# Causal masks by GpSimd affine select, one-column denominator weights, six product groups and a contiguous second quad, in a fused attention and MLP kernel

## The chip, the cores and the metric

The kernel runs on one core of a Trainium2 chip. The metric is the device time of one execution in microseconds (us); less is better. A time is the median of the runs of one kernel. A profiled execution has a span about 1.7 us shorter than its device time (before: 380.64 us and 378.9 us), so stage lengths below, which come from traces, add up to the span. On one core no second state could be told apart; every profiled run that is used here was classed fast.

The engines in the profile are PE (TensorE matmuls), PEld (TensorE weight loads), DVE (VectorE), ACT (ScalarE), POOL (GpSimd) and SP (SyncE, which issues most loads here). PSUM is the memory that TensorE writes its products to, SBUF the memory of everything else on the core.

## The reference, cut to what matters

```python
batch, n_heads, seq, head_dim = 8, 8, 576, 64        # f is in [0.8, 1.0)
def _attn_ref(q, k, v, f):
    scores = scale * q @ k^T                          # per batch and head
    cum = np.cumsum(np.log(np.clip(f, 1e-4, 1.0)), axis=-1)
    scores = np.where(causal, -1e9, scores + cum[..., :, None] - cum[..., None, :])
    attn = exp(scores - max);  attn = attn / sum(attn)
    return attn @ v
x = attention output as [4608, 512]                   # tokens by (head, dim)
h = x @ w_in                                          # w_in [512, 2048]
return gelu_tanh(h) @ w_out                           # w_out [2048, 512]
```

(Shortened; the mask, the decay and the division are as in the reference.)

## The kernel before: the parts that the change and the argument touch

The 64 heads are handled as 16 *quads* of four heads, two quads to a batch. A quad goes through four *rounds* of scores. In each, TensorE multiplies a strip of keys by queries, ScalarE takes the exp of it and writes it to `pt`, and the diagonal block of the strip is masked. The decay is folded into weights `w = exp(-cum)` of the keys: `vw = v * w` for the value product, `w` alone for the denominator. While quad `i` makes scores, the quad before it, `j`, makes its denominators and its two value products `po`, which VectorE multiplies by the reciprocal denominators into `xT`. Between these pieces, TensorE is kept busy with output matmuls of the MLP (`pull(fill, n)` pulls n of them). After every batch comes a block of MLP input matmuls (`mlp_in`) with Gelu on ScalarE.

```python
    rounds = [(0, [(0, 0, 400)]),
              (400, [(0, 400, 176), (3, 384, 192)]),
              (768, [(1, 128, 448)]),
              (1216, [(2, 256, 320), (4, 512, 64)])]
    po_parts = [(0, 256, 256), (256, 576, 512)]       # the product is cut where PSUM banks end
    # psS has 2 buffers of [128, 1024] FP32, psO has 1, psM has 2 of [128, 512]

    def make_vw(i):                                   # both on GpSimd
        nc.gpsimd.tensor_mul(vw[i % 2], v_nat[...], wT[:, i, :, :] ...broadcast)
        nc.gpsimd.tensor_copy(wrep[i % 2], wT[:, i, :, :] ...broadcast to 32 columns)

    def mask(i, r):                                   # of each diagonal block in round r
        nc.vector.tensor_mul(p[:, :, o:o + w], p[:, :, o:o + w], utri[:, :, :w] ...broadcast)

    def denominators(i):
        po = product(i, [... 32 equal columns of wrep for each head ...])
        nc.vector.transpose(out=den, in_=po)
        for x in range(2):
            nc.vector.reciprocal(rec[x], den[:, 0:S:32])
        for x in range(2):
            for g in (0, 64):                         # a head's rows to its neighbour's
                src, dst = g + 32 * x, g + 32 - 32 * x
                nc.vector.tensor_copy(rec[x][dst:dst + 32, :], rec[x][src:src + 32, :])
        # ... (cut) two transposes spread rec[x] to rb[x]

    def attn_out(i, x):                               # x: the pair of heads
        po = product(i, [... vw of two heads, 64 columns each ...])   # the one psO buffer
        nc.vector.tensor_mul(xT[b % 2][:, 2 * u + x, :], po, rbs.pop((i, x)))

    def step(i, j, fill, fills, n=None):              # i: scores, j: products, n: loads
        for r in range(4):
            # ... (cut) score_round(i, r): matmuls, two exps
            if j is not None and r > 0:
                if r == 1: denominators(j)
                else:      attn_out(j, r - 2)
            if r == 0:
                if n is not None: cast_k(n); cast_q(n)          # GpSimd
                if i is not None: make_vw(i)                    # GpSimd
            # ... (cut) transposes of k and q of quad n on VectorE in rounds 1 and 2
            if i is not None and r > 0: mask(i, r - 1)
            pull(fill, fills[r])
            if i is not None and r == 3: mask(i, 3)
```

The softmax here doesn't subtract the row's maximum and nothing guards it: scores larger than these inputs give would overflow.

## Time and profile before

Device time: 381.1 us, median of 3 runs (380.83 to 381.11).

The first thing to look at is how busy TensorE is in each stretch. The span falls into four: the start-up up to the end of the first MLP input block, the quads 2 to 4 up to the start of the second such block, the steady state up to the start of the last block, and the tail. This is the table of stretches of the kernel before: start and end, length, then busy time of each engine (with its number of instructions), the granted TensorE clock as a share of full speed, the share of the DMA engines, and GB/s.

```profile
core 0: us, PE busy (x) PEld busy (x) DVE busy (x) ACT busy (x) POOL busy (x), PEclk, DMA share, GB/s
0.00:61.43 61.43, 37.79 (x347) 24.25 (x348) 30.75 (x56) 27.39 (x37) 20.40 (x26) 0.92 1.12 191
61.43:92.58 31.15, 26.33 (x307) 12.32 (x314) 23.36 (x40) 21.56 (x27) 15.31 (x11) 0.95 0.81 170
92.58:340.21 247.63, 241.15 (x2373) 146.17 (x2401) 123.36 (x240) 146.59 (x197) 57.53 (x42) 1.00 0.44 97
340.21:378.90 38.69, 34.46 (x213) 20.95 (x214) 4.15 (x6) 10.32 (x16) 0.00 (x0) 0.98 0.11 41
```

TensorE is idle for 23.6 us of the first 61.4 (61.43 less 37.79), for 4.8 us of the next 31.2, and for 6.5 us of the long steady stretch. So the start-up holds the most that a change of order can win.

In the start-up the masks are the eye-catcher. These are two timelines of the kernel before, of VectorE and then of GpSimd (start, length, engine, line, operation, output and inputs, shapes, count; in brackets the idle time before it and what ended that).

```profile
19.13 0.63 DVE L193 TENSOR_TENSOR pt_91<-pt_91,utri 128x512 bf16<-128x512 bf16 x1
20.37 8.84 DVE L193 TENSOR_TENSOR pt_91<-pt_91,utri 128x512 bf16<-128x512 bf16 x4
```

```profile
20.38 2.34 POOL L160 TENSOR_TENSOR vw_89<-v_nat_83,wT 128x1280 bf16<-128x1280 f32 x1
22.66 0.93 POOL L163 CAST wrep_102<-wT 128x640 bf16<-128x640 f32 x1
...
25.84 2.36 POOL L160 TENSOR_TENSOR vw_90<-v_nat_83,wT 128x1280 bf16<-128x1280 f32 x1
28.12 0.95 POOL L163 CAST wrep_103<-wT 128x640 bf16<-128x640 f32 x1
```

Four masks take 8.84 us while GpSimd runs without a break (the cut line is its issue of three loads); one mask alone takes 0.38 us elsewhere. The Trainium skill, "GPSIMD Engine Reference", section 1. Specifications, says that GpSimd shares its SBUF interfaces with VectorE and contends with VectorE instructions of two SBUF inputs. A mask product has two SBUF inputs, and the trace agrees.

The end of the start-up is a serial piece with one PSUM tile. This is the timeline of all engines there:

```profile
41.39 0.72 DVE L242 TENSOR_TENSOR xT_93<-po,rb_463 128x576 bf16<-128x576 f32 x1
42.16 1.55 PE L208 MATMUL po<-pt_92,vw_90 128*64 128x256 bf16 x14 [1.75 <-DVE xT_93 L242]
43.74 0.76 DVE L242 TENSOR_TENSOR xT_93<-po,rb_465 128x576 bf16<-128x576 f32 x1 [1.64 <-PE po L208]
```

The second value product (at 42.16) can't start before the first multiply has read the only `po` tile, and the last `xT` is done at 44.50.

The table of waits (total us, times, longest) shows how long TensorE waited for such multiplies and for masks:

```profile
PE po L208 <- DVE xT_94 L242: 4.8, 6, 1.6
PE po L208 <- DVE xT_93 L242: 4.4, 3, 1.8
PE po L208 <- DVE pt_91 L193: 3.6, 3, 2.3
```

### The profile page before, as it was taken

Reading aid. Unit: us, or ns where it says so; the run is one execution under the profiler, and the core shown is the slowest. Engines: PE = TensorE matmul, PEld = TensorE weight load, DVE = VectorE, ACT = ScalarE, POOL = GpSimd, SP = SyncE. Lnnn points to the kernel's source line nnn. Section 1 sums busy time; section 2 is a strip of 40 time slices with the busy share of each in tenths; the row PEclk is TensorE's granted clock in tenths of the full one; section 3 lists DMA queues with packets and bytes.
Section 4 is the critical chain, followed back from the end, with each engine's and each line's share of the span. In section 5 each row is a group of like instructions: output and inputs, shape, how many; then the busy total and the mean of one; then the engine's idle time right before and its main releaser. Section 6 shows DMA issues by size and latency. Waiting matters only on the chain.

```text
span 378.9 us, 7775 instructions
## 1 busy us (share of the span) xinstructions
PE 339.7 (90%) x3235; PEld 203.7 (54%) x3273; DVE 181.6 (48%) x341; ACT 205.9 (54%) x276; POOL 93.2 (25%) x79
## 2 busy tenths in 40 slices
PE   0646698978999999999999999999999999899995
PEld 0214475435765467445754477446744576457742
DVE  4298502798307841396308840595128820760021
ACT  2744067746575556756674556655665557605500
POOL 1293115532501413050504131051406300000000
PEclk9999599989999999999999999999999999999999
DMA  9979999980692119911990239411911100010012
GB/s 186 204 113 195 216 221 219 229 189 29 161 205 67 57 57 222 153 50 39 213 190 29 83 101 220 93 49 67 226 18 55 57 29 0 29 57 28 2 55 83
DMA packets 86018, 42.59 MB, mean 112 GB/s; under 512 B 40352, under 2 KB 81312, under 8 KB 85984
## 3 DMA queue, kind: packets, MB, share of 16 engines
q1 hardware_dynamic: 79328, 36.73, 45.6%
q0 software_dynamic: 4224, 4.19, 7.0%
q10 hardware_dynamic: 2432, 1.18, 1.6%
q8 instruction: 25, 0.41, 0.5%
q14 instruction: 9, 0.07, 0.1%
HBM read 36.85 MB, written 9.44 MB: 122 GB/s over the span
## 4 chain that ended last, share of the span: by engine, by line
PE 75%; DVE 12%; issue 5%; DMA 4%; ACT 3%; SPq 0%; POOL 0%; ACTq 0%; POOLq 0%
PE ps_h L253 34%; PE pso L271 27%; PE po L208 9%; PE ps_s L175 5%; DVE pt_91 L193 2%; DMA v_nat_83<-in_v_dram 1%; DVE den L223 1%; DMA k_nat_80<-in_k_dram 1%; DVE xT_94 L242 1%; DVE pt_92 L193 1%; ACT pt_92 L184 1%; DMA k_nat_79<-in_k_dram 1%; DVE o_st L275 1%; ACT L184 1%; DVE xT_93 L242 1%
## 5 line engine op out<-in xcount | busy, mean ns | idle before, releaser
L271 PE MATMUL pso<-w_out_sb,gT 128*128 128x512 bf16 x538 | 129.2, 381 | 5.1 <-issue 4.6
L261 ACT ACTIVATE gT<-ps_h 128x576 bf16<-128x576 f32 x128 | 82.5, 651 | 75.9 <-PE ps_h L253 75.9
L253 PEld LDWEIGHTS <-w_in_sb 128*128 128x128 bf16 x1024 | 100.7, 98 | 29.5 <-issue 1.0
L271 PEld LDWEIGHTS <-gT 128*128 128x128 bf16 x576 | 51.6, 98 | 63.8 <-issue 8.4
L184 ACT ACTIVATE pt_91<-ps_s 128x800 bf16<-128x800 f32 (+3 forms) x64 | 50.1, 834 | 37.6 <-PE ps_s L175 30.0
L184 ACT ACTIVATE pt_92<-ps_s 128x800 bf16<-128x800 f32 (+3 forms) x64 | 50.1, 834 | 29.6 <-PE ps_s L175 21.6
L253 PE MATMUL ps_h<-xT_93,w_in_sb 128*128 128x288 bf16 x512 | 65.3, 289 | 0.5 <-ACT gT L261 0.5
L253 PE MATMUL ps_h<-xT_94,w_in_sb 128*128 128x288 bf16 x512 | 64.0, 286 | 0.1
L223 DVE STREAM_TRANSPOSE den<-po 128x576 f32<-128x576 f32 x16 | 12.5, 783 | 93.8 <-PE po L208 93.5
L275 DVE COPY o_st<-pso 128x512 f32<-128x512 f32 x36 | 24.7, 687 | 50.9 <-PE pso L271 46.4
L193 DVE TENSOR_TENSOR pt_92<-pt_92,utri 128x512 bf16<-128x512 bf16 (+1 forms) x40 | 30.9, 798 | 0.0
L193 DVE TENSOR_TENSOR pt_91<-pt_91,utri 128x512 bf16<-128x512 bf16 (+1 forms) x40 | 27.3, 718 | 4.6 <-ACT pt_91 L184 4.6
L147 POOL CAST k_bf<-k_nat_79 128x1152 bf16<-128x1152 f32 x8 | 9.2, 1148 | 80.5 <-DVE kT_88 L139 60.3
L175 PE MATMUL ps_s<-qT_85,kT_87 32*128 32x400 bf16 (+5 forms) x384 | 21.3, 299 | 7.6 <-DVE kT_87 L139 4.6
L175 PE MATMUL ps_s<-qT_86,kT_88 32*128 32x400 bf16 (+5 forms) x384 | 22.5, 294 | 2.7 <-DVE qT_86 L139 1.2
L160 POOL TENSOR_TENSOR vw_89<-v_nat_84,wT 128x1280 bf16<-128x1280 f32 x4 | 9.3, 2331 | 55.1 <-PE po L208 36.7
L175 PEld LDWEIGHTS <-kT_87 32*128 32x128 bf16 x384 | 8.1, 96 | 24.1 <-issue 17.7
L160 POOL TENSOR_TENSOR vw_89<-v_nat_83,wT 128x1280 bf16<-128x1280 f32 x4 | 9.3, 2335 | 45.2 <-PE po L208 36.1
L208 PE MATMUL po<-pt_91,vw_89 128*64 128x320 bf16 (+4 forms) x224 | 15.2, 278 | 5.1 <-DVE xT_94 L242 3.2
L208 PE MATMUL po<-pt_92,vw_90 128*64 128x320 bf16 (+4 forms) x224 | 15.3, 280 | 4.2 <-DVE xT_93 L242 1.8
L175 PEld LDWEIGHTS <-kT_88 32*128 32x128 bf16 x384 | 8.4, 95 | 19.4 <-issue 17.3
L208 PEld LDWEIGHTS <-vw_89 128*64 128x64 bf16 x224 | 11.5, 115 | 9.3 <-issue 8.4
(180 smaller groups left out, 230.2 us busy)
## 6 DMA issues: line engine op xcount, KB each, us to landing
out_dram<-o_st SPq DMA_DIRECT2D x36, 256.0 KB, 2.0
k_nat_79<-in_k_dram SPq DMA_DIRECT2D x32, 144.0 KB, 5.3
k_nat_80<-in_k_dram SPq DMA_DIRECT2D x32, 144.0 KB, 3.2
v_nat_84<-in_v_dram SPq DMA_DIRECT2D x16, 256.0 KB, 5.8
q_nat_77<-in_q_dram SPq DMA_DIRECT2D x28, 144.0 KB, 5.5
q_nat_78<-in_q_dram SPq DMA_DIRECT2D x28, 144.0 KB, 3.9
v_nat_83<-in_v_dram SPq DMA_DIRECT2D x12, 256.0 KB, 6.4
w_in_sb<-in_moe_w_in_dram POOLq DMA_DIRECT2D x4, 512.0 KB, 6.5
```

The source lines that it names most:

```text
L147: nc.gpsimd.tensor_copy(k_bf, k_nat[i % 2])
L160: nc.gpsimd.tensor_mul(vw[i % 2], v_nat[(i // QPB) % 2][:, :, h0:h0 + 4, :], wT[:, i, :, :].unsqueeze(3).to_broadcast([128, NT, 4, D]))
L175: nc.tensor.matmul(tiles[h // 2][:, h % 2, c0:c0 + nq], kk[32 * h:32 * h + 32, 128 * t:128 * t + 128, c], qq[32 * h:32 * h + 32, q0:q0 + n ...
L184: nc.scalar.activation(p[:, 2 * g:2 * g + 2, off:off + n], tiles[g][:, :, 0:n], AF.Exp, scale=scale)
L193: nc.vector.tensor_mul(p[:, :, o:o + w], p[:, :, o:o + w], utri[:, :, :w].to_broadcast([128, 4, w]))
L208: nc.tensor.matmul(po[r0:r0 + w.shape[-1], base + s - a:base + z - a], w, p[:, h, strip_off[t] + s - 128 * t:strip_off[t] + z - 128 * t], ...
L223: nc.vector.transpose(out=den, in_=po)
L242: nc.vector.tensor_mul(xT[b % 2][:, 2 * u + x, :], po, rbs.pop((i, x)))
L253: nc.tensor.matmul(ph[:, j, 0:hS], w_in_sb[:, dt, 128 * ft:128 * ft + 128], xT[b % 2][:, dt, hS * j:hS * (j + 1)], start=(dt == 0), stop=( ...
L261: nc.scalar.activation(gT[:, ft, o:o + S].rearrange("p (j n) -> p j n", j=2), ph[:, :, 0:hS], AF.Gelu_apprx_tanh)
L271: nc.tensor.matmul(pso, gT[:, ft, c:c + 128], w_out_sb[:, ft, :], start=(ft == 0), stop=(ft == N_FT - 1))
L275: nc.vector.tensor_copy(st, pso)
```

## The change

It takes the masks off VectorE (GpSimd makes them by affine select, which has one input), drops the 32-column weight copies `wrep` for one bf16 column per head, moves the denominators from round 1 to round 0, cuts a value product into six groups of matmuls in place of seven (64 + 512 columns in place of 256 + 320 at the bank boundary), gives the last start-up step a spare PSUM tile, and loads the second quad's k and q contiguously, cast to bf16 on the way, so that no cast is needed. The loads of quad 3 go ahead of v of batch 1. The diff, cut to its core:

```diff
-    po_parts = [(0, 256, 256), (256, 576, 512)]
+    Q0 = S - 512
+    po_parts = [(0, Q0, 512 - Q0), (Q0, S, 512)]
+    def load_contiguous(src, dst, i):            # one GpSimd DMA per tensor, FP32 to BF16
+    def transpose_contiguous(src, dst):          # (bodies cut)
 def make_vw(i): ...
-        nc.gpsimd.tensor_copy(wrep[i % 2], wT[:, i, :, :] ... [128, NT, 4, 32])
 def mask(i, r): ...
-                nc.vector.tensor_mul(p[:, :, o:o + w], p[:, :, o:o + w], utri[...])
+                nc.gpsimd.affine_select(
+                    out=p[:, :, o:o + w], in_=p[:, :, o:o + w], compare_op=ALU.is_ge,
+                    fill=0.0, base=0, pattern=[[0, 4], [1, w]], channel_multiplier=-1)
-    def product(i, groups):
-        po = psO.tile([128, 1024], FP32, name="po", tag="po")
+    def product(i, groups, spare):
+        if spare: po = psS.tile([128, 2, 512], FP32, name="ps_o", tag="s") ...
+        else:     po = psO.tile([128, 1024], FP32, name="po", tag="po")
 def denominators(i): ...
+        # weights: one column of w_bf, spread to 32 columns for t == 0 only
         for x in range(2):
+            rec = den_pool.tile([128, S // 32], FP32, ...)
+            nc.vector.reciprocal(rec, den[:, 0:S:32])
             for g in (0, 64):
-                nc.vector.tensor_copy(rec[x][dst:dst + 32, :], rec[x][src:src + 32, :])
+                nc.vector.tensor_copy(rec[dst:dst + 32, :], rec[src:src + 32, :])
             # then the transpose of this x into rb (before: after both pairs of copies)
 def step(...): ...
-            if j is not None and r > 0:
-                if r == 1: denominators(j)
-                else:      attn_out(j, r - 2)
+            if j is not None:
+                if r == 0:  denominators(j)
+                elif r > 1: attn_out(j, r - 2, spare=(i is None and r == 2))
...
-                fills = (11, 8, 8, 9) if b % 2 else (9, 6, 6, 7)
+                fills = (8, 11, 8, 9) if b % 2 else (6, 9, 6, 7)
```

(Cut: the setup's order of loads, two calls of `transpose_contiguous` and `make_vw(0)` in round 1 of the first step, the other fill counts, `load_qk(3)` moved up.)

More of the change, by code (lines that the diff above doesn't have):

```diff
@@ L73 @@
     ones_f32 = singles.tile([128, 128], FP32, name="ones_f32")
-    utri = singles.tile([128, 1, 128], BF16, name="utri")
     q_nat = many(2, [128, NA, 2, D], FP32, "q_nat")
@@ L82 @@
     kT = many(2, [128, SPAD, 2], BF16, "kT")
+    qk_c = many(2, [128, S // 32, D], BF16, "qk_c")
     vw = many(2, [128, NT, 4, D], BF16, "vw")
@@ L92 @@
     wT = singles.tile([128, NQ, NT, 4], FP32, name="wT")
-    wrep = many(2, [128, NT, 4, 32], BF16, "wrep")
+    w_bf = singles.tile([128, NQ, NT, 4], BF16, name="w_bf")
     shift = singles.tile([128, 1], FP32, name="shift")
@@ L144, in transpose_one @@
         )
+    def load_contiguous(src, dst, i):
+        b, h0 = i // QPB, 4 * (i % QPB)
+        return nc.gpsimd.dma_start(
+            out=dst.rearrange("p a d -> p (a d)"),
+            in_=src[b, h0:h0 + 4].rearrange("h (p a) d -> (h p) (a d)", p=32))
+    def transpose_contiguous(src, dst):
+        nc.vector.transpose(
+            out=dst[:, 0:S, :].rearrange("p s c -> p (s c)").bitcast(FP32)
+                .rearrange("p (t a) -> p a t", a=S // 32),
+            in_=src.rearrange("p a d -> p (a d)").bitcast(FP32)
+                .rearrange("p (a d) -> p a d", d=D // 2),
+        )
     def cast_k(i):
@@ L162, in make_vw @@
             wT[:, i, :, :].unsqueeze(3).to_broadcast([128, NT, 4, D]))
-        nc.gpsimd.tensor_copy(
-            wrep[i % 2], wT[:, i, :, :].unsqueeze(3).to_broadcast([128, NT, 4, 32]))
     def score_round(i, r):
@@ L192, in mask @@
                 w = min(128, nq)
-                nc.vector.tensor_mul(p[:, :, o:o + w], p[:, :, o:o + w],
-                                     utri[:, :, :w].to_broadcast([128, 4, w]))
-    def product(i, groups):
-        po = psO.tile([128, 1024], FP32, name="po", tag="po")
+                nc.gpsimd.affine_select(
+                    out=p[:, :, o:o + w], in_=p[:, :, o:o + w], compare_op=ALU.is_ge,
+                    fill=0.0, base=0, pattern=[[0, 4], [1, w]], channel_multiplier=-1)
+    def product(i, groups, spare):
+        if spare:
+            po = psS.tile([128, 2, 512], FP32, name="ps_o", tag="s").rearrange("p a n -> p (a n)")
+        else:
+            po = psO.tile([128, 1024], FP32, name="po", tag="po")
         p = pt[i % 2]
@@ L210, in product, with column, attn_out @@
                         p[:, h, strip_off[t] + s - 128 * t:strip_off[t] + z - 128 * t],
-                        start=(t == 0), stop=(t == (1 if z == 256 else 4)),
+                        start=(t == 0), stop=(t == (0 if z == Q0 else 4)),
                         skip_group_check=True,
                     )
-        return po[:, 256:256 + S]
+        return po[:, 512 - Q0:512 - Q0 + S]
     rbs = {}
     def denominators(i):
-        po = product(i, [(32 * g, lambda t, h=h: wrep[i % 2][:, t, h, :], h)
-                         for g, h in enumerate((0, 2, 1, 3))])
+        def column(h):
+            return lambda t: (w_bf[:, i, t, h:h + 1] if t else
+                              w_bf[:, i, t, h:h + 1].to_broadcast([128, 32]))
+        po = product(i, [(32 * g, column(h), h) for g, h in enumerate((0, 2, 1, 3))], False)
         den = den_pool.tile([128, S], FP32, name="den", tag="den")
         nc.vector.transpose(out=den, in_=po)
-        rec = [den_pool.tile([128, S // 32], FP32, name=f"rec{x}", tag=f"rec{x}") for x in range(2)]
         for x in range(2):
-            nc.vector.reciprocal(rec[x], den[:, 0:S:32])
-        for x in range(2):
+            rec = den_pool.tile([128, S // 32], FP32, name=f"rec{x}", tag=f"rec{x}")
+            nc.vector.reciprocal(rec, den[:, 0:S:32])
             for g in (0, 64):
                 src, dst = g + 32 * x, g + 32 - 32 * x
-                nc.vector.tensor_copy(rec[x][dst:dst + 32, :], rec[x][src:src + 32, :])
-        for x in range(2):
+                nc.vector.tensor_copy(rec[dst:dst + 32, :], rec[src:src + 32, :])
             rb = den_pool.tile([128, S], FP32, name=f"rb{x}", tag=f"rb{x}")
             nc.vector.transpose(out=rb.rearrange("p (c j) -> p c j", j=32),
-                                in_=rec[x].unsqueeze(2).to_broadcast([128, S // 32, 32]))
+                                in_=rec.unsqueeze(2).to_broadcast([128, S // 32, 32]))
             rbs[i, x] = rb
-    def attn_out(i, x):
+    def attn_out(i, x, spare=False):
         b, u = i // QPB, i % QPB
         po = product(i, [(64 * y, lambda t, h=2 * x + y: vw[i % 2][:, t, h, :], 2 * x + y)
-                         for y in range(2)])
+                         for y in range(2)], spare)
         nc.vector.tensor_mul(xT[b % 2][:, 2 * u + x, :], po, rbs.pop((i, x)))
@@ L286, in setup @@
         nc.sync.dma_start(out=f_sb, in_=f.rearrange("b h s -> (b h) s"))
-        load_heads(k, k_nat, 0, nc.sync)
+        k0 = load_heads(k, k_nat, 0, nc.sync)
         load_heads(q, q_nat, 0, nc.scalar)
         load_v(0, 0, 4)
-        load_heads(k, k_nat, 1, nc.sync)
         load_v(0, 4, 4)
@@ L293, in setup @@
         make_upper_triangular(nc, utri_f32, val=1.0, diag=True)
+        after(load_contiguous(k, qk_c[1], 1), k0[0])
+        load_contiguous(q, qk_c[0], 1)
         cast_k(0)
@@ L301, in setup @@
             nc.vector.memset(t_[:, S:SPAD, :], 0.0)
-        nc.vector.tensor_copy(utri[:, 0, :], utri_f32)
         nc.vector.tensor_scalar(f_sb, f_sb, 1e-4, 1.0, op0=ALU.max, op1=ALU.min)
@@ L306, in setup @@
         nc.scalar.activation(f_sb, f_sb, AF.Ln)
-        load_heads(q, q_nat, 1, nc.scalar)
         ps_lt = psM.tile([128, NT * BH], FP32, name="ps_lt", tag="m")
@@ L332, in make_w @@
                 AF.Exp, scale=-1.0, bias=shift[:rows, :])
+        nc.vector.tensor_copy(w_bf, wT)
     def pull(it, n):
@@ L350, in step @@
                     make_w()
-            if j is not None and r > 0:
-                if r == 1:
+            if j is not None:
+                if r == 0:
                     denominators(j)
-                else:
-                    attn_out(j, r - 2)
+                elif r > 1:
+                    attn_out(j, r - 2, spare=(i is None and r == 2))
             if r == 0:
@@ L361, in step @@
                     w_in_dmas.append(load_w_in(0))
-                if i is not None:
+                elif i is not None:
                     make_vw(i)
@@ L368, in step @@
                     transpose_q(n)
+            if i == 0 and r == 1:
+                make_vw(0)
+                transpose_contiguous(qk_c[1], kT[1])
+                transpose_contiguous(qk_c[0], qT[1])
             if i is not None and r > 0:
@@ L390 @@
         setup()
-        step(0, None, none, (0, 0, 0, 0), n=1)
+        step(0, None, none, (0, 0, 0, 0))
         w_in_dmas.extend(load_w_in(c) for c in range(1, 4))
@@ L395 @@
         step(1, 0, none, (0, 0, 0, 0))
+        load_qk(3)
         w_out_dmas = [load_w_out(c) for c in range(4)]
@@ L398 @@
         after(v1[0], w_out_dmas[1])
-        load_qk(3)
         step(None, 1, none, (0, 0, 0, 0))
@@ L419 @@
                 load_qk(5)
-                step(3, 2, fill, (7, 3, 3, 3), n=4)
+                step(3, 2, fill, (3, 7, 3, 3), n=4)
                 load_qk(6)
-                step(4, 3, fill, (6, 2, 2, 2))
+                step(4, 3, fill, (2, 6, 2, 2))
             elif b + 1 < B:
                 i = 2 * b + 3
-                fills = (11, 8, 8, 9) if b % 2 else (9, 6, 6, 7)
+                fills = (8, 11, 8, 9) if b % 2 else (6, 9, 6, 7)
                 pull(fill, 2)
@@ L430 @@
                 else:
-                    step(None, i, fill, (7, 6, 7, 7))
+                    step(None, i, fill, (6, 8, 6, 7))
         for x in fill:
```

## The prediction

> **What bounds the kernel now.** By stage (the table of stretches, PE busy of length): 0 to 43.6 us, start-up, PE 20.4 of 43.6; 43.6 to 61.5, first MLP-in, 17.4 of 17.9; 61.5 to 94, quads 2 to 4 between the first output tiles, 27.7 of 32.5; 94 to 342, steady state, about 97% (41.3 of 42.0, 39.6 of 41.0); 342 to 379, pure MLP tail. So after 94 us it is TensorE throughput, and what can be won lies before 94 us.
>
> Start-up, in the timeline: the second quad's k lands at 17.1, its scores start at 20.5. Then the five DVE masks of quad 0 end at 29.2 (four take 8.84 us, though one alone takes 0.38), because GpSimd is busy 9.98 of those 10 us. This agrees with the Trainium skill, "GPSIMD Engine Reference", section Specifications: GpSimd shares SBUF interfaces with VectorE and contends with instructions of two SBUF inputs, which a mask product is. The denominator matmuls wait for these masks and hold quad 1's round 2 until 29.44. After the last exp (34.4) the masks, denominator, two value products through one PSUM tile and two multiplies run in series until 44.5.
>
> **What changes.**
> 1. Masks go to GpSimd. The trace's own affine selects (0.23 us for 64 columns, 0.29 for 128) give an estimate of 0.5 to 0.75 us for 512 columns. DVE loses about 58 us busy; GpSimd gains about 50, loses 13.7 (weight copies). Start-up: quad 0's masks end at about 22 in place of 29.2, quad 1's last exp at about 30 in place of 34.4.
> 2. Spare PSUM tile: the second value product no longer waits 1.75 us for the multiply. Last xT at about 38 in place of 44.5: -6.5 us.
> 3. Contiguous loads: fewer, larger packets. Casting loads with larger pieces moved about 316 GB/s of source against 212 for the small-packet queue, so the 1.18 MB quad saves about 2 us of transfer; quad 1 is ready before PE wants it.
> 4. Six groups and one-column weights: successive product matmuls already start N/2.4 ns apart (320 columns 132 ns, 128 columns 52), weight loads are hidden. A product of seven groups takes 0.81 us against 0.67 for its 1600 columns. I expect 10 to 20 ns per product, 0.5 to 1 us in all.
> 5. Denominators one round earlier: the multiplies stop holding the PSUM tile. PE waits for xT (4.8 us after 61 us in the table of waits) mostly vanish: -3 us in 61 to 94, about -0.3 us a period later. GpSimd masks of round 3 now stand just ahead of the denominators: margin 0 to 0.4 us, so perhaps small new waits.
> 6. Quad 3's loads go ahead of v of batch 1. DMA runs without a break to 82 us; I expect v near 61 us, while MLP-in ends near 55. make_vw, and behind it on GpSimd the masks of quad 2, wait for it: about 1.5 us given back.
>
> **Sum:** -6.5 (start-up), -3+1.5 (quads 2 to 4), -2.5 (steady state), -0.7 (groups): about -11. Predicted 370.0 us, 80% range 365.0 to 374.5. Chances: faster by over 2% 0.84, within 2% 0.15, slower 0.01.
>
> **What the profile would show.** First MLP-in block done near 55 us (61.4 before); end of stage three near 84 to 86 (94); steady periods 0.3 to 0.6 us shorter; the tail still 37 us; affine selects about 0.7 us; PE waits on xT gone; PE waiting on masks near 66 us; product 0.79 to 0.81 us.
>
> **What would make it wrong.** Affine selects of 1 us or more, so that denominators wait in every round; first loads delayed because the contiguous ones stand ahead of the first GpSimd cast; DMA order starving v or the output weights by more than 2 us; or a colder clock in start-up.

## More of the kernel before

```profile
110.18 0.65 ACT L261 ACTIVATE gT<-ps_h 128x576 bf16<-128x576 f32 x1 [0.33 <-PE ps_h L253]
110.85 1.28 ACT L184 ACT_TABLE_LOAD   x1
112.15 1.57 ACT L184 ACTIVATE pt_92<-ps_s 128x800 bf16<-128x800 f32 x2
```

The table load of 1.28 us starts right after the last Gelu, without a wait. (The Trainium skill, "ScalarE: Activation LUTs", section What ACT_TABLE_LOAD costs, gives about 1283 ns for the load; the trace agrees.)

## The result

| | before | after |
|---|---|---|
| median, us | 380.99 (380.83 to 381.11, 4 runs) | 374.6 (374.07 to 375.21, 4 runs) |
| ratio to before | 1 | 0.9833 (95%: 0.9813 to 0.9853) |

A ratio here is the mean time of one kernel's fast runs over that of the other's fast runs of the same rounds, so it is not quite the ratio of the medians beside it. The kernel became 1.7% faster, which counts as the same at the 2% line. The prediction was 370.0 us, with a chance of 0.84 for more than 2%, and 374.6 lies just outside its range of 365.0 to 374.5.

This is the table of stretches of the kernel after, cut at the same events as before and with the same columns.

```profile
0.00:54.85 54.85, 36.60 (x331) 21.83 (x332) 23.01 (x46) 27.39 (x37) 23.87 (x35) 1.00 1.04 187
54.85:87.68 32.83, 27.26 (x292) 11.51 (x297) 16.41 (x28) 20.28 (x26) 17.11 (x19) 0.90 0.92 188
87.68:334.70 247.02, 241.49 (x2277) 140.44 (x2305) 95.33 (x182) 147.86 (x198) 82.43 (x90) 1.00 0.43 97
334.70:373.40 38.70, 34.52 (x214) 20.95 (x214) 4.15 (x6) 10.30 (x16) 0.00 (x0) 0.98 0.11 41
```

Set beside the prediction:

| stage | before, us | after, us | measured change | predicted change |
|---|---|---|---|---|
| start-up | 61.43 | 54.85 | -6.58 | -6.5 |
| quads 2 to 4 | 31.15 | 32.83 | +1.68 | -3 + 1.5 = -1.5 |
| steady | 247.63 | 247.02 | -0.61 | -2.5 - 0.7 = -3.2 |
| tail | 38.69 | 38.70 | 0 | 0 |
| span | 378.9 | 373.4 | -5.5 | -11.2 |

The start-up came out as predicted. The two middle stages are 3.2 and 2.6 us worse than predicted, and these 5.8 us are what has to be explained.

Now the lines that answer to those shown of before. The end of the start-up, in the timeline of all engines:

```profile
34.26 1.54 PE L227 MATMUL ps_o<-pt,vw 128*64 128x64 bf16 x12
35.62 1.50 PE L227 MATMUL po<-pt,vw 128*64 128x64 bf16 x12
38.08 0.72 DVE L264 TENSOR_TENSOR xT<-ps_o,rb 128x576 bf16<-128x576 f32 x1
38.72 0.74 DVE L264 TENSOR_TENSOR xT<-po,rb 128x576 bf16<-128x576 f32 x1
```

The two products now follow each other, and the last `xT` is done at 39.46 instead of 44.50.

From the table of waits, the one of TensorE for multiplies:

```profile
PE po L227 <- DVE xT L264: 5.3, 3, 2.9
```

The waits for masks are gone. Of the waits of the products (`po`) for `xT`, 9.2 us before (4.4 + 4.8), 5.3 are left. The same table by stage says where: in the start-up they fell from 4.4 to 2.4 us and in the steady stage from 2.0 to none, but in the stage of quads 2 to 4 they went from 2.8 us (1.6 and 1.2) to 2.9, in one piece. Around that one, in the stage of quads 2 to 4, the timeline of all engines shows:

```profile
67.72 1.15 POOL L166 CAST q_bf<-q_nat 128x1152 bf16<-128x1152 f32 x1
...
68.16 3.03 DVE L254 COPY rec<-rec 32x18 f32<-32x18 f32 x2
...
68.83 2.33 POOL L176 TENSOR_TENSOR vw<-v_nat,wT 128x1280 bf16<-128x1280 f32 x1
...
74.93 0.74 DVE L264 TENSOR_TENSOR xT<-po,rb 128x576 bf16<-128x576 f32 x1
...
75.72 1.55 PE L227 MATMUL po<-pt,vw 128*64 128x64 bf16 x12 [2.93 <-DVE xT L264]
```

In the kernel before, the same pair of copies came while GpSimd had nothing to do (it had been idle for 9.13 us when its next product started at 81.74), and took 0.35 us:

```profile
76.33 0.35 DVE L231 COPY rec_870<-rec_870 32x18 f32<-32x18 f32 x2
...
81.74 2.33 POOL L160 TENSOR_TENSOR vw_89<-v_nat_83,wT 128x1280 bf16<-128x1280 f32 x1 [9.13 <-DMA q_nat_77<-in_q_dram]
```

After, two copies of 32 x 18 numbers take 3.03 us. In the trace the first ends at 68.89, 0.02 us after the cast of q (67.72 + 1.15 = 68.87). The second runs from 68.90 to 71.19, and the product that makes `vw` ends at 71.16. Behind them the whole chain to the multiply at 74.93 is late, TensorE waits 2.93 us, and its clock drops: the value product after the wait takes 1.55 us, where the one at 70.34 took 0.87. The view by source line gives the spread of this copy's duration over the kernel (min/median/max in ns):

```profile
L254 DVE COPY rec<-rec x64: 164/171/2290, 24.6 to 329.8; 32x18 f32<-32x18 f32 x64
```

In the steady state, the timeline of ScalarE at the switch of its function table from Gelu to Exp:

```profile
105.28 0.65 ACT L283 ACTIVATE gT<-ps_h 128x576 bf16<-128x576 f32 x1 [0.33 <-PE ps_h L275]
106.44 1.28 ACT L198 ACT_TABLE_LOAD   x1 [0.50 <-PE ps_s L189]
107.73 0.84 ACT L198 ACTIVATE pt<-ps_s 128x800 bf16<-128x800 f32 x1
```

The load of the Exp table now starts 0.5 us after the last Gelu, only when the scores are there. Before, it started without a wait.

### The profile page after: what moved, and what is told of

Read it like the earlier page. It is cut to its first block, busy times and chain, and to the rows that moved or that the text cites. A ratio compares the mean times of both kernels' runs of the same rounds, so it can differ in the third digit from the quotient of the medians.

```text
span 373.4 us, 7488 instructions
## 1 busy us (share of the span) xinstructions
PE 339.9 (91%) x3108; PEld 194.7 (52%) x3145; DVE 138.9 (37%) x261; ACT 205.8 (55%) x276; POOL 123.4 (33%) x143
## 4 chain that ended last, share of the span: by engine, by line
PE 84%; DVE 6%; ACT 4%; issue 3%; DMA 2%; POOL 0%; ACTq 0%
PE ps_h L275 33%; PE pso L293 31%; PE po L227 9%; PE ps_s L189 9%; ACT pt L198 3%; DVE rec L254 2%; DMA k_nat<-in_k_dram 1%; DVE rb L256 1%; DVE xT L264 1%; DMA q_nat<-in_q_dram 1%; DVE den L247 1%; PE cum_ps L347 0%; DVE o_st L297 0%; ACT gT L283 0%; DVE rec L251 0%
## 5 line engine op out<-in xcount | busy, mean ns | idle before, releaser
L198 ACT ACTIVATE pt<-ps_s 128x800 bf16<-128x800 f32 (+3 forms) x128 | 100.2, 834 | 68.3 <-PE ps_s L189 66.0
L275 PE MATMUL ps_h<-xT,w_in_sb 128*128 128x288 bf16 x1024 | 128.2, 286 | 1.6 <-DVE xT L264 1.1
L208 POOL TENSOR_SCALAR_AFFINE_SELECT pt<-pt 128x512 bf16<-128x512 bf16 (+1 forms) x80 | 46.2, 591 | 158.0 <-ACT pt L198 156.3
L189 PE MATMUL ps_s<-qT,kT 32*128 32x400 bf16 (+5 forms) x768 | 44.7, 297 | 11.9 <-ACT pt L198 6.1
L176 POOL TENSOR_TENSOR vw<-v_nat,wT 128x1280 bf16<-128x1280 f32 x16 | 37.5, 2342 | 10.8 <-DMA v_nat<-in_v_dram 4.8
L264 DVE TENSOR_TENSOR xT<-po,rb 128x576 bf16<-128x576 f32 x30 | 22.7, 755 | 35.7 <-PE po L227 35.7
L227 PE MATMUL po<-pt,vw 128*64 128x64 bf16 (+1 forms) x360 | 28.9, 300 | 4.5 <-DVE xT L264 4.5
L227 PEld LDWEIGHTS <-vw 128*64 128x64 bf16 x384 | 17.2, 118 | 19.0 <-issue 13.0
L256 DVE STREAM_TRANSPOSE rb<-rec 128x576 f32<-128x576 f32 x32 | 24.9, 778 | 1.1
L254 DVE COPY rec<-rec 32x18 f32<-32x18 f32 x64 | 18.5, 290 | 1.5
```

What stands on the lines that cost most here:

```text
L176: nc.gpsimd.tensor_mul(vw[i % 2], v_nat[(i // QPB) % 2][:, :, h0:h0 + 4, :], wT[:, i, :, :].unsqueeze(3).to_broadcast([128, NT, 4, D]))
L189: nc.tensor.matmul(tiles[h // 2][:, h % 2, c0:c0 + nq], kk[32 * h:32 * h + 32, 128 * t:128 * t + 128, c], qq[32 * h:32 * h + 32, q0:q0 + n ...
L198: nc.scalar.activation(p[:, 2 * g:2 * g + 2, off:off + n], tiles[g][:, :, 0:n], AF.Exp, scale=scale)
L208: nc.gpsimd.affine_select(out=p[:, :, o:o + w], in_=p[:, :, o:o + w], compare_op=ALU.is_ge, fill=0.0, base=0, pattern=[[0, 4], [1, w]], ch ...
L227: nc.tensor.matmul(po[r0:r0 + w.shape[-1], base + s - a:base + z - a], w, p[:, h, strip_off[t] + s - 128 * t:strip_off[t] + z - 128 * t], ...
L254: nc.vector.tensor_copy(rec[dst:dst + 32, :], rec[src:src + 32, :])
```

## The experiments

Theories before the first experiments:

- *Held copies.* The copies between the two halves of `rec` on VectorE are held by whatever GpSimd runs at that moment. With the change they come at the moment at which GpSimd casts and makes `vw`. The Trainium skill, "SBUF — State Buffer", section Who interferes with whom, says that a copy can enter a mode that uses the port pair shared with GpSimd, and that the pair is an exclusive lock: whichever instruction starts first keeps it to its end, and the other is blocked. The end times above agree.
- *Load order* (the prediction's own reason, and the rival for the stage of quads 2 to 4). v of batch 1 comes later, so `vw` and the masks behind it on GpSimd come later.
- *Late table load* against *denominators that gain nothing* and *groups that gain nothing*, for the steady state.

Where the quoted expectations use letters, A is the held copies, B the load order, C the late table load, and D and E, which were formed later, say that the engine of the masks matters little (D) or much (E) in the start-up. All twelve kernels gave the right result. Each has four timed runs. Stage lengths are from the profiled run of each (us); the median and ratio are of the timed runs. These twelve kernels were run in three sessions on three chips, where the kernel before took 381.25, 380.93 and 380.87 us, so medians of different sessions compare to about 0.4 us.

| kernel | start-up | quads 2 to 4 | steady | median | ratio to before (95%) |
|---|---|---|---|---|---|
| before | 61.43 | 31.15 | 247.63 | 380.99 | 1 |
| after | 54.85 | 32.83 | 247.02 | 374.6 | 0.9833 (0.9813 to 0.9853) |
| e1_no_copies | 53.53 | 28.27 | 247.04 | 369.31 | 0.9686 (0.9672 to 0.9701) |
| e7_vw_later | 53.74 | 30.15 | 247.03 | 370.39 | 0.9722 (0.9702 to 0.9742) |
| e6_v_first | 54.50 | 32.17 | 247.03 | 375.15 | 0.9847 (0.9788 to 0.9906) |
| e2_early_table | 55.49 | 31.12 | 245.05 | 371.79 | 0.9739 (0.9709 to 0.9768) |
| e5_den_later | 54.02 | 33.21 | 249.69 | 377.71 | 0.9913 (0.9848 to 0.9978) |
| e3_seven_groups | 56.94 | 32.06 | 247.06 | 376.05 | 0.9859 (0.9829 to 0.9889) |
| e4_dve_masks | 53.41 | 32.54 | 259.01 | 387.62 | 1.0169 (1.0121 to 1.0217) |
| e8_both | 51.82 | 28.49 | 245.05 | 366.27 | 0.9625 (0.9586 to 0.9663) |
| e9_both_dve_later | 55.31 | 33.31 | 252.00 | 381.33 | 1.0007 (0.9975 to 1.0039) |
| e10_both_strided | 55.75 | 28.75 | 245.06 | 370.71 | 0.9734 (0.9710 to 0.9757) |
| e11_both_seven | 53.87 | 27.59 | 245.09 | 367.04 | 0.9637 (0.9613 to 0.9661) |
| e12_both_no_spare | 56.27 | 27.62 | 245.12 | 369.30 | 0.9704 (0.9679 to 0.9729) |

The steady stage is the same to 0.1 us between kernels that differ only elsewhere (247.02 to 247.06, and 245.05 to 245.12), so a difference of 2 us there is large. The first two stages are noisier, because the clock in the start-up differs between runs: e11 and e8 do the same work there but for the groups, and their start-ups differ by 2.05 us (twelve MLP matmuls took 2.92 us in e11, 1.63 in e8). A start-up of one profiled run that is 2 us longer shows nothing by itself.

### e1_no_copies: no copy can be held

On top of the kernel after, the neighbour's rows are made by a reciprocal that reads the denominators again, instead of by a copy of the reciprocals. The values are the same.

```diff
-                nc.vector.tensor_copy(rec[dst:dst + 32, :], rec[src:src + 32, :])
+                nc.vector.reciprocal(rec[dst:dst + 32, :], den[src:src + 32, 0:S:32])
```

> The changed kernel, with each 32-row copy of the reciprocals replaced by a second reciprocal straight from the transposed denominators. Theory A (the copies are held by GpSimd): the reciprocals are not held (0.2 to 0.3 us each), the 2.9 us wait of TensorE for xT near 73 us falls to under 0.5 us and the cold clock after it goes; the stretch from the end of the first MLP-in block to the start of the second falls from 32.8 us to 28 to 30; start-up about 1 us shorter; 374.6 falls to 369 to 371.5. Rival B (the load order of v, and the queue of GpSimd work behind it, costs the time): the wait for xT stays over 2 us and the time within 1 us of 374.6.

Measured: 369.31 us, 5.3 us less than after (374.6 - 369.31). The stage of quads 2 to 4 went from 32.83 to 28.27 us, the start-up from 54.85 to 53.53, and the steady stage did not move. First the view by source line, then the timeline of all engines, of this kernel:

```profile
L254 DVE RECIPROCAL rec<-den x64: 254/258/264, 24.5 to 324.2; 32x18 f32<-32x18 f32 x64
```

```profile
67.90 2.33 POOL L176 TENSOR_TENSOR vw<-v_nat,wT 128x1280 bf16<-128x1280 f32 x1
...
68.70 0.53 DVE L254 RECIPROCAL rec<-den 32x18 f32<-32x18 f32 x2
...
71.99 0.88 PE L227 MATMUL po<-pt,vw 128*64 128x64 bf16 x12 [0.28 <-DVE xT L264]
```

The pair at 68.70 runs wholly inside GpSimd's `vw` product and takes 0.53 us, as ever. The reciprocal is the slower instruction when both are free (0.26 us against 0.17), but it is never held, and TensorE's wait falls from 2.93 to 0.28 us. This stage now gains 2.9 us on the kernel before (31.15 - 28.27), which is what the prediction had given it without the load order.

### e7_vw_later: keep the copies, move what holds them

If e1 had helped for another reason than the hold, the copies could stay. Here they do, and GpSimd's `vw` product of quads 1 and 3 is issued at the end of the step instead.

```diff
-                elif i is not None:
+                elif i is not None and i not in (1, 3):
                     make_vw(i)
 ...
                 mask(i, r - 1)
+            if r == 3 and i in (1, 3):
+                make_vw(i)
```

> The changed kernel, copies kept, but the GpSimd product of values and weights of quads 1 and 3 is issued after the third mask of its step in place of before the first. Theory A: the long GpSimd instruction no longer lies over the copies, so both long copy pairs (2.78 and 3.03 us) fall to under 1.5 us (casts or affine selects may still hold one), and the time falls by 2 to 4 us, to 370.5 to 372.5. Rival B: no change, 374 to 375.

Measured: 370.39 us, 4.2 us less than after. The timeline of all engines:

```profile
67.90 1.14 POOL L166 CAST q_bf<-q_nat 128x1152 bf16<-128x1152 f32 x1
...
68.28 1.38 DVE L254 COPY rec<-rec 32x18 f32<-32x18 f32 x2
...
73.77 0.87 PE L227 MATMUL po<-pt,vw 128*64 128x64 bf16 x12 [0.94 <-DVE xT L264]
```

The first copy of the pair is now held by the cast of q (it ends at 69.07, the cast at 69.04) and the second by an affine select (69.67; the select ends at 69.63). The pair takes 1.38 us in place of 3.03, and TensorE's wait, 0.94 us, is between those of e1 and of after. e1 and e7 share nothing but the hold: one removes the held instruction, the other most of the holder. The held copies are shown.

### e6_v_first: the load order undone

```diff
         step(1, 0, none, (0, 0, 0, 0))
-        load_qk(3)
         w_out_dmas = [load_w_out(c) for c in range(4)]
         v1 = load_v(1)
         after(v1[0], w_out_dmas[1])
+        load_qk(3)
```

> The changed kernel with the loads of quad 3 behind those of v of batch 1 again. Rival B (the load order costs the time): v lands near 55 us, the GpSimd queue runs ahead, and the time falls to 371 to 372.5. Theory A: quad 3's casts stand ahead of the product of values and weights in GpSimd's queue and now land last, near 60 us, so GpSimd's work falls on the same places; a copy is still held and the time stays within 1 us of 374.6.

Measured: 375.15 us (372.55 to 377.21, a noisy set), no better than after. In its trace the copies are still held, 3.09 us at 67.86, and TensorE still waits 3.04 us for `xT`. The stage went from 32.83 to 32.17 us. So the load order costs nothing that these runs can show, and the rival falls for the kernel after. (On the repaired kernel e8 it was not tested.) In the kernel after, v did land near 60 us, as predicted, and the masks of quad 2 ended at 66.68; but the denominator product, which had started at 66.12, did not wait for them.

### e2_early_table: the table load as early as before

A one-column exp, issued right after the last Gelu of a block, makes ScalarE load the Exp table without waiting for scores.

```diff
+    prime = singles.tile([128, 1], FP32, name="prime")
 ...
             fill = mlp_out(out_tiles(b))
+            if b + 1 < B:
+                nc.scalar.activation(prime, shift, AF.Exp)
```

> The changed kernel, with one dummy Exp of one column on ScalarE after the last GELU of each MLP-in block but the last, which waits for nothing of TensorE. Theory C: in the changed kernel the load of the Exp table waits 0.5 us for the first scores after each block, which it did not before, and the second score round pays for it; with the dummy the load follows the last GELU at once, the second score round of each step loses 0.25 to 0.5 us of wait, and the time falls by 1.5 to 3 us, to 371.6 to 373.1. If the wait is hidden elsewhere: under 0.5 us.

Measured: 371.79 us, 2.8 us less than after; the steady stage 245.05 in place of 247.02. The timeline of ScalarE:

```profile
104.22 0.65 ACT L284 ACTIVATE gT<-ps_h 128x576 bf16<-128x576 f32 x1 [0.33 <-PE ps_h L276]
104.89 1.28 ACT L445 ACT_TABLE_LOAD   x1
106.18 0.20 ACT L445 ACTIVATE prime<-shift 128x1 f32<-128x1 f32 x1
```

The load again follows the last Gelu without a wait. In the table of waits of the steady stretch, the kernel after has TensorE's second score round waiting for exps 3 times, 1.4 us in all, and ScalarE waiting in front of the table load 6 times, 3.0 us in all. Both entries are absent in this kernel.

Why the load came late with the change: in the kernel before, an exp had to wait for VectorE (the masks of the quad that used the same `pt` buffer before) and for TensorE. My reading is that the table load stood after the first wait and ahead of the second, so it ran while the scores were made; with the masks on GpSimd no wait for VectorE is left in front, and the load stands behind the wait for TensorE. The traces do not show the order of these waits. They do show which part of the change matters: in e4 (masks back on VectorE, early denominators kept) all six table loads of the steady stage start right after the last Gelu, the first at 104.23 us; in e5 (masks on GpSimd, denominators back) all six wait 0.50 us. So it is the move of the masks. That the late load costs 2.0 us is shown by this run.

### e5_den_later: the denominators back in round 1

```diff
             if j is not None:
-                if r == 0:
+                if r == 1:
                     denominators(j)
 ...
-                fills = (8, 11, 8, 9) if b % 2 else (6, 9, 6, 7)
+                fills = (11, 8, 8, 9) if b % 2 else (9, 6, 6, 7)
```

(The other fill counts go back in the same way.)

> The changed kernel with the denominators in the second round again, and the old numbers of output matmuls per round. By the prediction (step 5) this gives back 2.5 us in the steady state and 3 us before 94 us: 378 or more. By the traces the steady state has only 0.3 us in every second period to give back and the early stretch loses or gains with where GpSimd holds the copies: 373.5 to 376.5, start of second to start of last MLP-in block 246.5 to 248.

Measured: 377.71 us, 3.1 us more than after. The steady stage is 249.69, so the early denominators gain 2.7 us there, about what the prediction gave them (2.5); my expectation from the traces, 246.5 to 248, fell. The copies are held here too (2.19 us at 69.43), and TensorE waits 4.2 us for `xT` in quads 2 to 4 (2.9 in after). So it is not the earlier round that brings the copies under GpSimd's work. The sum of the steady stage agrees: 247.63 before, plus 2.0 for the late table is 249.6, against 249.69 measured here; less 2.7 for the early denominators is 247.0, against 247.02 after. The gain was real, and the late table took most of it back. The sum is a check and not a test: e9 below, which should come out near 247.6 by it, is at 252.00.

### e3_seven_groups: the product cut as before

```diff
-    Q0 = S - 512
+    Q0 = 256
 ...
-                        start=(t == 0), stop=(t == (0 if z == Q0 else 4)),
+                        start=(t == 0), stop=(t == (1 if z == Q0 else 4)),
```

> The changed kernel with the products cut at column 256 again (seven groups, as before the change). By the prediction (10 to 20 ns per product, 48 products) it would be 0.5 to 1 us slower. By the traces (0.808 against 0.807 us per value product) it is the same within 0.2 us. Correct either way.

Measured: 376.05 us, but the steady stage is 247.06 against 247.02: no gain from the six groups. What is slower is the start-up of the profiled run (56.94 against 54.85), where a pair of copies fell on a cast of k (1.20 us), TensorE then waited 2.14 us for `xT` (1.13 in after), and its next twelve matmuls took 2.86 us (1.63 in after). That is the held copies again, and the clock, not the groups. So the sum of the whole time was of no use for this question, and the stage was. From start to start, a value product takes 0.808 us before and 0.807 after.

### e4_dve_masks: masks back on VectorE, early denominators kept

```diff
-                nc.gpsimd.affine_select(
-                    out=p[:, :, o:o + w], in_=p[:, :, o:o + w], compare_op=ALU.is_ge,
-                    fill=0.0, base=0, pattern=[[0, 4], [1, w]], channel_multiplier=-1)
+                nc.vector.tensor_mul(p[:, :, o:o + w], p[:, :, o:o + w],
+                                     utri[:, :, :w].to_broadcast([128, 4, w]))
```

> The changed kernel with the masks on VectorE again, as products with two SBUF inputs. If the move of the masks is what gained the start-up: masks of quad 0 are held by the GpSimd product, end later than 22 us by 2 us or more, and the time is 376 to 380. If the start-up gain came from the other parts (contiguous load, no weight copies and casts on GpSimd, earlier denominators): 373.5 to 375.5. The steady state is the same within 0.3 us per period either way, since VectorE has slack there.

Measured: 387.62 us, 13.0 us more than after, of which 12.0 lie in the steady stage (259.01 against 247.02), although the table load is early again there. My expectation that the steady stage would stay fell. From the table of waits of this kernel, and then from its timeline of VectorE:

```profile
PE po L226 <- DVE pt L208: 13.4, 16, 1.5
```

```profile
114.79 0.76 DVE L263 TENSOR_TENSOR xT<-po,rb 128x576 bf16<-128x576 f32 x1 [2.00 <-PE po L226]
115.46 1.98 DVE L208 TENSOR_TENSOR pt<-pt,utri 128x512 bf16<-128x512 bf16 x1
```

The denominators of round 0 need the masks of the quad's last round. On VectorE these stand behind a multiply, and GpSimd holds them (1.98 us for one here, while a `vw` product runs from 114.83 to 117.16). TensorE waits for them 16 times, 12 of them in the steady stage (9.0 us). The start-up, though, was as fast as that of e1 (53.41): the masks' engine alone is not what made the start-up quick.

### e8_both: the two repairs together

e1 and e2 in one kernel, with no other edit.

> The changed kernel with both repairs: second reciprocals in place of the copies, and the dummy Exp. If the two losses are separate (one lies before the second MLP-in block, the other in each period after it), the gains add: 369.3 less 2 to 2.8, so 366.4 to 367.5, and the stretch from the start of the second to the start of the last MLP-in block falls from 247.0 to 245.0 us. If they overlap: 368.5 or more.

Measured: 366.27 us (365.88 to 367.78), ratio 0.9625 to before: 8.3 us less than after. The two gains add (5.3 + 2.8 = 8.1). Of the steady stage its table of stretches shows that TensorE is idle for only 0.3 us of 245:

```profile
80.31:325.36 245.05, 244.72 (x2306) 140.22 (x2305) 97.26 (x182) 148.41 (x204) 82.58 (x90) 1.00 0.43 98
```

This must not be set against the 6.5 us of the kernel before. The trace of e8 has 2306 matmuls in this stage, those of after and e2 have 2277 and 2278. After and e2 have the 24 short gaps (3.8 us) that the kernel before also has, and e8 has none, yet the stage is as long in e2 as in e8 (245.05). So the gaps are missing records, and what the kernel before could win here was 6.5 less 3.8, or 2.7 us, about the 2.6 that e8 won.

This version beats both kernels. The four runs that follow each undo one part of the change on top of it.

### e9_both_dve_later: masks on VectorE and denominators in round 1, with both repairs

The edits are those of e4 and e5, on e8.

> The twice repaired kernel with the masks on VectorE and the denominators in the second round, both as before the change; contiguous load, spare PSUM tile, six groups and repairs stay. Theory D: in the start-up the masks' engine matters little, since the casts and weight copies that held the masks are gone from GpSimd there; the first MLP-in block ends within 1.5 us of the twice repaired kernel's 51.8 us. In the steady state the early denominators are missing, so start of second to start of last MLP-in block is 247 to 248 us in place of 245.05. In all 368.5 to 371. Rival E (moving the masks is what gained the start-up): the block ends at 55 us or later, and the time is 372 or more.

Measured: 381.33 us, 15.1 us more than e8, where I had expected 368.5 to 371. The start-up is 3.5 us longer than that of e8, quads 2 to 4 are 4.8 us longer, and the steady stage 7.0. From its timeline of VectorE:

```profile
76.33 4.46 DVE L209 TENSOR_TENSOR pt<-pt,utri 128x512 bf16<-128x512 bf16 x3
```

Masks that GpSimd holds are back, and TensorE waits for `xT` 12 times, 11.9 us in all (2 times and 1.1 us in e8). So the move of the masks, together with the early denominators that it makes possible, is worth 15 us in the repaired kernel. My sizes for it fell by 10 us. The start-up of 55.31 us is what rival E had asked for (55 or later), but it stays open what the masks alone are worth there: the denominators moved too, e4 had a short start-up with its masks on VectorE, and part of the difference is clock (twelve MLP matmuls took 2.80 us, 1.63 in e8). Why the steady stage here is 4.4 us longer than even the kernel before (252.00 against 247.63) isn't settled: the chain of reciprocals is longer (0.53 us a pair against 0.35) and in another order than before, and no run tells these apart.

### e10_both_strided: the second quad loaded in pieces and cast, as before

```diff
         load_v(0, 0, 4)
+        load_heads(k, k_nat, 1, nc.sync)
 ...
-        after(load_contiguous(k, qk_c[1], 1), k0[0])
-        load_contiguous(q, qk_c[0], 1)
 ...
+        load_heads(q, q_nat, 1, nc.scalar)
```

(And the cast and transposes of quad 1 go back into the first step.)

> The twice repaired kernel with the second quad's k and q loaded head by head, cast on GpSimd and transposed as before the change. The two casts (2.3 us) stand in GpSimd's queue ahead of the masks of quad 0, and the smaller packets cost about 2 us of transfer: the masks of quad 0 end 1 to 2.5 us later, the first MLP-in block ends 1 to 3 us later than 51.8 us, the steady state is unchanged, the time 367.3 to 369.5. If the contiguous load is worth nothing: within 0.5 us of 366.3.

Measured: 370.71 us, 4.4 us more than e8 (I had expected 1 to 3). The start-up is 3.9 us longer. From the timeline of GpSimd:

```profile
17.04 1.15 POOL L164 CAST k_bf<-k_nat 128x1152 bf16<-128x1152 f32 x1 [7.08 <-DMA k_nat<-in_k_dram]
18.13 1.15 POOL L167 CAST q_bf<-q_nat 128x1152 bf16<-128x1152 f32 x1
...
22.46 2.76 POOL L209 TENSOR_SCALAR_AFFINE_SELECT pt<-pt 128x512 bf16<-128x512 bf16 x5
```

GpSimd waits 7.08 us for k and then has two casts to do, ahead of the `vw` product and the masks of quad 0, which end at 25.2. In e8 they end at 21.5. The `vw` product starts 5.8 us later than in e8 (20.18 against 14.39): for 2.65 of these, k had not landed, and the casts take 2.2. So the contiguous load seems to pay because it takes both, the late k and the casts, out of GpSimd's queue in front of the masks that it now makes. This is read from the timeline; neither was tested by itself.

### e11_both_seven: seven groups, with both repairs

The edit is that of e3, on e8.

> The twice repaired kernel with seven groups, so that no held copy falls differently. By the traces the groups are worth nothing: within 0.4 us of 366.3, steady state 245.0 to 245.2. By the prediction 0.5 to 1 us slower. If the seven-group run on the changed kernel (1.45 us slower) told of the groups themselves: 367.3 or more.

Measured: 367.04 us against 366.27, with 95% intervals of the ratios that overlap, and a steady stage of 245.09 against 245.05. The 0.77 us between the medians is more than the 0.4 that I had allowed, but the profiled runs differ only in the first two stages, where the clock differs (see above). In the steady stage the groups are worth nothing that can be measured.

### e12_both_no_spare: no spare PSUM tile, with both repairs

```diff
-                    attn_out(j, r - 2, spare=(i is None and r == 2))
+                    attn_out(j, r - 2)
```

> The twice repaired kernel without the spare PSUM tile: in start-up the second value product of quad 1 waits for the first multiply again, about 1.6 us (1.75 before the change), and once more before the last MLP-in block, where output matmuls lie between. First MLP-in block about 1.6 us later, time 367.5 to 368.5.

Measured: 369.30 us, 3.0 us more than e8 (I had expected 1.2 to 2.2). From its timeline of TensorE:

```profile
37.27 1.55 PE L228 MATMUL po<-pt,vw 128*64 128x64 bf16 x12 [2.29 <-DVE xT L265]
```

The wait that the spare tile takes away is back, and the product after it ran at half speed (1.55 us; in e8 the two products of this place took 0.88 each). The start-up is 4.4 us longer, and the next stage 0.9 shorter. That a cold clock adds to the wait is read from these durations, not tested by itself.

## Why the prediction was wrong, point by point

1. *What bounds the kernel: right.* What could be won did lie mostly before 94 us. But the kernel before also had about 2.6 us to win in the steady stage (247.63 against 245.05 in e8), and I treated 97% busy as the limit there (and part of the missing 3% were missing records).
2. *Masks on GpSimd: right.* An affine select of 128 x 512 took 0.635 us (estimate: 0.5 to 0.75). The masks of quad 0 ended at 22.1 us (predicted 22) and the last exp of quad 1 at 30.4 (predicted 30).
3. *Spare tile and start-up: right.* -6.58 us against -6.5, but that the sum fits so well is partly luck. The -6.5 was to be the gain of the last `xT`, at about 38; it was done at 39.46, 5.04 us earlier than before. The other 1.54 lie behind it: the first sixteen MLP matmuls took 3.41 us in the kernel before, and after it four ran ahead of the last `xT` (0.66 us) and twelve took 1.63. The 112 that follow took 13.88 us in both. e12 and e10 show that the spare tile and the contiguous load each carry a part (3.0 and 4.4 us on the repaired kernel, more than I had thought).
4. *Six groups, "0.5 to 1 us in all": wrong.* Nothing was measured in the steady stage (e3, e11). My estimate took 1600 columns at the speed of the streams, 0.67 us for a product, as within reach of fewer groups. The product took 0.807 us with six groups too. The start times of the matmuls in the traces say why. From the first group of a product to its last it is 679 ns in both kernels. The first group takes 25 to 26 ns more than its columns need at 2.4 a ns, however many they are (133 ns for 256 columns before, 52 for 64 after; 2.4 columns a ns is the speed that the prediction had read off the trace), and each later one 2 to 6 ns more, so one group less saves next to nothing. The rest, 0.13 us, follows the start of the last group.
5. *Denominators one round earlier: this is the step that failed.* The prediction put it so: "the multiplies stop holding the PSUM tile. PE waits for xT (4.8 us after 61 us in the table of waits) mostly vanish: -3 us in 61 to 94, about -0.3 us a period later." In the steady stage the earlier denominators are indeed worth 2.7 us (e5), and the waits for `xT` are gone there (2.0 us before). In the stage of quads 2 to 4, where 3 us were forecast, the waits stayed: 2.8 us before, 2.9 after. What I left out is what VectorE's instructions behind the denominators meet when the stage starts 6.6 us earlier. GpSimd's work for quad 3, which comes behind waits for loads, stayed where it was (cast of k at 66.37 before and 66.63 after, `vw` product at 69.42 and 68.83), while the copies of the reciprocals came forward from 76.33 to 68.16. So they now fall on GpSimd's cast and `vw` product and are held 3.03 us (e1: 5.3 us on the whole kernel, 4.6 in this stage; e7: 4.2). The earlier round has little part in it: with the denominators back in round 1 (e5) the copies come at 69.43 and are held too. I had cited the shared interfaces for the masks, and did not ask which of the remaining VectorE instructions could be held. In the steady stage the gain came, but the Exp table load now waits for the scores and takes 2.0 us of it back (e2).
6. *Load order, "about 1.5 us given back": wrong.* v landed when I said, but in the kernel after nothing waited for it: no wait of TensorE for masks near 66 us, and e6 gained nothing. In e8, where TensorE gets to this point 3.4 us earlier, one wait for a mask is there, of 0.3 us.
7. *The sum.* Predicted stage by stage: -6.5, -1.5, -3.2. Measured: -6.6, +1.7, -0.6. The 3.2 us of the second stage are the held copies (4.6 by e1), less the 1.5 us that the load order was to cost and did not. The 2.6 us of the third are the late table (2.0) and the groups that gave nothing (0.7), less the 0.2 by which the early denominators did better than predicted (2.7 against 2.5).

## What to carry to other kernels

When a change moves work between VectorE and GpSimd, list every VectorE instruction that remains, down to the smallest copy, and ask what GpSimd will be running when each of them comes. Ask it again for every stage that will start earlier, because work of another engine that waits for loads need not move with it. A copy of 0.17 us held up to 2.3 us can undo the gain if a PSUM tile hangs on it. After removing a wait of an engine, look at what had been done behind that wait: here a function table load seems to have been hidden there, and a dummy activation put it back in its place. Compare by stages cut at the same events; the whole time mixed a gain of 6.6 us with losses that had other causes, and hid that the groups gain nothing.

## What the Trainium skill lacked or had wrong

- "SBUF — State Buffer", Who interferes with whom, names copies, casts and tensor-scalar instructions as able to take the shared pair. It doesn't name the reciprocal, and no other page that I found says of it whether it is held. Here 64 reciprocals of 32 x 18 took 254 to 264 ns, also under GpSimd instructions, where 64 copies took 164 to 2290 ns (e1 and after).
- "GPSIMD Engine Reference", section 1. Specifications, names the contention but not its size, nor that it lasts for the other's whole instruction. That is on the SBUF page, and a reader of the engine's page can miss it, as I did: 2.29 us for a copy of 0.17.
- "ScalarE: Activation LUTs", What ACT_TABLE_LOAD costs, does not say where a load falls among the waits of the activation that needs it. In the steady stage it ran free where VectorE made the masks (before and e4) and waited 0.50 us for the scores each time where GpSimd made them (after and e5), worth 2.0 us over the stage (after against e2).
- The same section adds about 1380 ns of drain to each switch, about 2.66 us in all. In these traces a switch took 1.3 us: the load ended at 107.72 and the exp started at 107.73, and in front of the load there was no gap where nothing had to be waited for (110.83 to 110.85 in the kernel before).
- "GPSIMD Engine Reference" has no duration for an affine select. Here it was 0.635 us for 128 x 512 and 0.415 us for 128 x 256, bf16.
- "TensorE: Matmul & The Clock Gate", HAM trace caveats, warns that the clock records are unreliable. The runs agree: the record of the kernel after grants 1.00 from 30 to 36 us, while its value products there took 1.54 us, as in the run of e2, whose record says 0.50; in e8, also recorded as 1.00, they took 0.88. The length of a known product is the better witness.
